# State exchange and a two-layer FFN in float32: batch 1, batch 7 and the state rows move from dense products to block products

## The chip, the cores and the metric

One core of a Trainium2 chip. The metric is the device time in microseconds (us) of one execution, from the runs of the whole program.

## The reference

The attention part reads a state of 32 rows per head and writes it back; the result feeds a two-layer network.

```python
B, H, S, D = x.shape                      # 8, 8, 512, 64; state has 32 rows
a = softmax(scale * x @ state.T)          # over the 32 state rows
xread = a @ state
a2 = softmax(scale * state @ x.T)         # over the 512 tokens
sread = a2 @ x
y = concat([xread, sread], axis=2).transpose(0, 2, 1, 3).reshape(B * 544, 512)
h = y @ w_in                              # 512 x 2048
g = where(h >= 1, h, where(h <= -1, 0, (h + 1) ** 2 / 4))
out = g @ w_out                           # 2048 x 512
```

So there are 8 x 512 token rows and 8 x 32 = 256 state rows. All is float32. TensorE takes each operand as a high and a low part (the low part is the operand less its rounded high part), and each product is three matmuls: high x high, high x low, low x high.

## The kernel before, in words

**First product.** `xread` is never formed. For each batch and each 256 columns of `w_in`, the state is multiplied by `w_in` (small matmuls of 32 x 256, line 639, the S steps), split into high and low (`sw_0h`, `sw_0l`, lines 653 and 655), and multiplied by the attention weights `ath`, `atl` (lines 698 to 700, the U steps). ACT and DVE turn the result into g: `relu` (L707), `square` (L711), `bound` (L715), then, where g feeds a dense product, its high and low part (L724, L730).

**Second product.** Batches 0 and 1 use it densely: `g2` (lines 751 to 753, 192 matmuls of 512 columns a batch, the G steps). Batches 2 to 7 go in pairs (2,3), (4,5), (6,7) through block products in the manner of Strassen and Winograd: per pair 7 products of blocks instead of 8, in two groups of channels g. The Q steps (`quarter`, line 1296, name Q g.k.n) are 336 matmuls of 512 columns a pair. `operand_ops` makes block operands (DVE sums, and a high and a low part each), `weight_ops` loads 1024 KB blocks of W_out (the tile `blocks` in DRAM) through SP, and `done_ops` adds the products up. The 256 state rows come last: their first product has 256 columns (L steps, lines 698 to 700 on `sath`, `satl`), their second is dense (M steps, 96 matmuls of 512 columns), with W_out reloaded by the W steps. `finish` (L764) copies their result out in two parts, one on ACT (L769), one on DVE (L767), and stores each in four pieces of 64 KB from the queues of SP and ACT.

**W_out's block sums.** The D steps (`block_ops`, line 1190) store W_out's split parts in `blocks`, add high and low part on DVE into a work place (`whole`, L1202), make four block sums there (L1208 to L1211), split them (L1214, L1218) and store them too:

```python
nc.vector.tensor_tensor(out=place()[:, :1024], in0=flat[:, 0], in1=flat[:, 1], op=ALU.add)
```

**Attention.** Scores (L480, X steps), then on DVE a 32 x 32 transpose (`turn`, L491), maximum, subtraction, sum, division, transpose back and low part in pieces of 512 elements; the other direction takes a maximum over tokens (`top2`, L560), exchanges through DRAM (`e_there`, `e_x`) and ends in the state read (`read2`, L603, the R steps).

**Order.** The stage of loading (batch 0 and the weights' decoding, lines 781 to 825) follows `ORDER`, a list of numbered operations with their engine. Behind it, `STEPS` lists PE's order step by step, and the class `Flow` places all the other engines' operations around it by costs and buffer rooms. Every engine and every DMA queue works its list in order. `warm` (L401) fills PE with matmuls without a use before the first product.

Of the kernel before, what the change touches and what calls it, by code (L numbers as in the profile page):

```python
# [8 lines left out]
F32 = mybir.dt.float32  # L9
# [9 lines left out]
PAD = 96  # L19
# [297 lines left out]
def state_exchange_moe(  # L317
# [130 lines left out]
    def trade_in(there, name):  # L448

        traded = work.tile([P, NPR, 2 * P], F32, tag="tmp", name=f"{name}_x")  # L450
        for t in range(NT):
            nc.sync.dma_start(
                out=traded[t * NS:(t + 1) * NS], in_=there[:, t].rearrange("(r n) k -> n r k", n=NS)
            )
        return traded

    class Attention:


# [1041 lines left out]
```

## Time and profile before

| what | us |
|---|---|
| runs: lowest, median, highest of 3 | 610.61, 612.99, 613.44 |
| the profiled execution | 610.56 |
| its span, from the first to the last instruction | 608.4 |
| PE, DVE, ACT busy | 600.7, 497.3, 391.5 |
| DMA moved | 122.27 MB, mean 201 GB/s |

The span lies inside the execution's time. An engine's busy time counts each instruction from its start to its modelled end; where they are pipelined, the distance from start to start (the pitch) is shorter than the duration. PEld stands for TensorE's weight loads, SPq for SP's DMA queue. "Idle before" a group names what the engine waited for.

### The profile page before, as it was taken

To read this page: it belongs to the slowest core of one execution; us is meant where nothing else is said; L and a number is where in the kernel's file an instruction comes from. 1 tells how busy PE (TensorE), PEld (TensorE's weight loads), DVE (VectorE), ACT (ScalarE), POOL (GpSimd) and SP (SyncE) were. 2 spreads that over 40 slices of the span, in tenths; PEclk is the share of its full clock that TensorE was granted. 3 is DMA by queue.
4 is the path that set the end of the run, shared out by engine and by line. 5 is a ranking of instruction groups with operands and counts; after the bars stand their busy time and mean duration, and the time that the engine had idled before them with its cause. 6 is when DMAs were issued, how large, how long until landed. Compare 5 with 4: busy or idle time off the path is not lost.

```text
span 608.4 us, 10010 instructions
## 1 busy us (share of the span) xinstructions
PE 600.7 (99%) x4154; PEld 476.6 (78%) x4154; DVE 497.3 (82%) x574; ACT 391.5 (64%) x480; POOL 0.8 (0%) x7
## 2 busy tenths in 40 slices
PE   8999999999999999999999999999999999999997
PEld 3677777787777777878787887788788878888885
DVE  6999985998999999998799849997688484995530
ACT  6999866565589674885566576865656576554520
POOL 0000000000000000000000000000000000000000
PEclk9999999999999999999999999999999999999999
DMA  8997258959474659324587436324646442435971
GB/s 354 424 425 250 69 176 326 371 207 364 149 257 171 229 149 325 81 71 138 163 294 246 129 100 213 105 69 139 208 141 206 139 139 70 138 123 194 358 293 35
DMA packets 65420, 122.27 MB, mean 201 GB/s; under 512 B 2912, under 2 KB 51680, under 8 KB 59232
## 3 DMA queue, kind: packets, MB, share of 16 engines
q1 hardware_dynamic: 65040, 121.32, 56.7%
q8 instruction: 32, 0.52, 0.3%
q10 hardware_dynamic: 336, 0.33, 0.2%
q14 instruction: 12, 0.10, 0.0%
HBM read 91.23 MB, written 30.41 MB: 200 GB/s over the span
## 4 chain that ended last, share of the span: by engine, by line
PE 94%; DVE 2%; ACT 2%; DMA 1%; SPq 0%; issue 0%
PE bank L1296 38%; PE bank L698 11%; PE bank L699 10%; PE bank L700 10%; PE bank L751 6%; PE bank L752 6%; PE bank L753 6%; PE bank L639 5%; PE bank L603 1%; PE bank L480 1%; DMA f<-in_moe_w_in_dram 1%; ACT f L804 1%; ACT f L796 1%; DVE w L812 1%; DVE r L730 0%; DVE one L715 0%
## 5 line engine op out<-in xcount | busy, mean ns | idle before, releaser
L1296 PE MATMUL bank<-r,r 128*128 128x512 f32 x1008 | 238.0, 391 | 0.0
L1296 PEld LDWEIGHTS bank<-r,r 128*128 128x128 f32 x1008 | 188.0, 188 | 44.3 <-issue 4.1
L1262 ACT CAST r<-f 128x1024 fp32r<-128x1024 f32 x84 | 86.9, 1050 | 48.7 <-PE bank L1296 21.8
L707 ACT ACTIVATE f<-bank,half 128x512 f32<-128x512 f32 x104 | 70.9, 687 | 68.3 <-PE bank L700 66.5
L1238 DVE TENSOR_TENSOR r<-f,r 128x1024 fp32r<-128x1024 f32 x84 | 101.3, 1217 | 14.1 <-ACT r L1262 13.8
L715 DVE SCALAR_TENSOR_TENSOR f<-f,bank 128x1024 f32<-128x1024 f32 x52 | 63.0, 1214 | 33.2 <-ACT f L711 33.2
L751 PE MATMUL bank<-r,r 128*128 128x512 f32 x160 | 63.0, 394 | 0.0
L752 PE MATMUL bank<-r,r 128*128 128x512 f32 x160 | 62.3, 389 | 0.0
L753 PE MATMUL bank<-r,r 128*128 128x512 f32 x160 | 62.3, 389 | 0.0
L711 ACT ACTIVATE f<-f 128x1024 f32<-128x1024 f32 x52 | 55.1, 1062 | 1.3
L1330 DVE TENSOR_TENSOR one<-one,bank 128x1024 f32<-128x1024 f32 x30 | 36.4, 1214 | 16.9 <-PE bank L1296 16.1
L1238 DVE TENSOR_TENSOR f<-f,f 128x1024 f32<-128x1024 f32 x36 | 43.4, 1218 | 0.1
L751 PEld LDWEIGHTS bank<-r,r 128*128 128x128 f32 x160 | 30.0, 188 | 9.4 <-issue 2.1
L753 PEld LDWEIGHTS bank<-r,r 128*128 128x128 f32 x160 | 30.0, 188 | 6.4
L752 PEld LDWEIGHTS bank<-r,r 128*128 128x128 f32 x160 | 30.0, 188 | 6.0
L639 PE MATMUL bank<-w,sb 64*32 64x256 f32 x1024 | 32.9, 380 | 1.5 <-DVE w L812 1.0
L639 PEld LDWEIGHTS bank<-w,sb 64*32 64x32 f32 x1024 | 17.6, 106 | 13.4 <-issue 4.0
L707 ACT ACTIVATE one<-bank,half 128x512 f32<-128x512 f32 (+1 forms) x25 | 19.6, 805 | 11.9 <-DVE r L730 8.8
L724 ACT CAST r<-one 128x1024 fp32r<-128x1024 f32 (+1 forms) x17 | 17.0, 999 | 10.4 <-PE bank L752 5.8
L715 DVE SCALAR_TENSOR_TENSOR one<-one,bank 128x1024 f32<-128x1024 f32 (+1 forms) x17 | 19.6, 1150 | 2.2 <-ACT one L711 1.9
L1332 ACT COPY one<-bank 128x1024 f32<-128x1024 f32 x12 | 12.2, 1013 | 13.4 <-PE bank L1296 13.4
L730 DVE TENSOR_TENSOR r<-one,r 128x1024 fp32r<-128x1024 f32 (+1 forms) x17 | 19.7, 1157 | 1.3 <-ACT r L724 1.2
(197 smaller groups left out, 977.1 us busy)
## 6 DMA issues: line engine op xcount, KB each, us to landing
r<-blocks SPq DMA_DIRECT2D x50, 1024.0 KB, 5.8
xt<-in_xt_dram SPq DMA_DIRECT2D x16, 512.0 KB, 6.3
f<-in_moe_w_in_dram SPq DMA_DIRECT2D x8, 1024.0 KB, 10.7
f<-in_moe_w_out_dram SPq DMA_DIRECT2D x8, 1024.0 KB, 14.5
blocks<-r SPq DMA_DIRECT2D x8, 1024.0 KB, 8.9
blocks<-f SPq DMA_DIRECT2D x8, 1024.0 KB, 5.3
xn<-in_x_dram SPq DMA_DIRECT2D x7, 1024.0 KB, 8.8
out_dram<-one SPq DMA_DIRECT2D x12, 512.0 KB, 5.4
```

Source lines behind the costliest of these rows:

```text
L639: nc.tensor.matmul(banks[hh][pr * NS:(pr + 1) * NS, cols], lhsT=sb[rows, b, pr], rhs=w32[c][rows, pr], start=True, stop=True,)
L698: nc.tensor.matmul(o, lhsT=wh[:, k, sl], rhs=ah[:, k], start=first, stop=False)
L699: nc.tensor.matmul(o, lhsT=wl[:, k, sl], rhs=ah[:, k], start=False, stop=False)
L700: nc.tensor.matmul(o, lhsT=wh[:, k, sl], rhs=al[:, k], start=False, stop=last)
L707: nc.scalar.activation(out=u, in_=h, func=AF.Relu, scale=0.5, bias=half)
L715: nc.vector.scalar_tensor_tensor(out=u, in0=u, scalar=1.0, in1=h, op0=ALU.min, op1=ALU.max)
L751: nc.tensor.matmul(a, lhsT=lh, rhs=oh, start=f == 0, stop=False)
L752: nc.tensor.matmul(a, lhsT=lh, rhs=ol, start=False, stop=False)
L753: nc.tensor.matmul(a, lhsT=ll, rhs=oh, start=False, stop=f == NF - 1)
L1238: tt = lambda o, a, b, f: nc.vector.tensor_tensor(out=o, in0=a, in1=b, op=f)
L1262: op(("hi", g, k, half), "ACT", 0.97, lambda: nc.scalar.copy(out=view()[:, 0], in_=value()), need, take=[("win", win)], ends=ends)
L1296: nc.tensor.matmul(o, lhsT=lhs, rhs=v[:, e, a], start=fresh and n == m == 0, stop=n == 3 and m == 2, skip_group_check=not fresh,)
```

## The change

- Batch 1 leaves the dense second product. The pairs are now (1,2), (3,4), (5,6). Batch 7 and the 256 state rows form a block product of their own: 768 rows in two sides of 384 (`SIDE`, `wide`), 336 matmuls of 384 columns. The M and W steps are gone; the state rows' first product (L steps) writes into the block product's bases.
- W_out's high and low part are no longer added on DVE. SP copies the stored high part from `blocks` into the place (`wa`), then POOL adds the stored low part by a DMA that accumulates (`wb`), 512 KB each, eight times; the sums on DVE wait for it.
- Attention pieces of batches 1 to 7 take 1024 elements instead of two of 512. Batch 0 is split by halves of its tokens instead of by halves of its heads.
- The state reads with their exchange are moved: those of batches 0 and 1 out of the loading stage, all of them to other places. The row loads of batches 0 and 1 move with them.
- The warm matmuls run behind the first scores, not ahead of them. `ORDER` and `STEPS` are new.
- The last additions are made in two halves of 384 columns, the second of which ACT's queue stores. The output has another layout, which is undone outside of the timed program.

```diff
-            op(("dA", c), "SP", 2.6, lambda: store_block(0, rounded(wo_at[c]).bitcast(F32)), [("wol", c)], ends=[("wo", c)])
-            op(("wa", c), "DVE", 1.14, whole, [("wol", c), ("send", 0, 3)], take=[("s", ("s", c))], ends=[("wo", c)])
-            op(("ws", c), "DVE", 1.5, sums, [("wa", c)])
+            op(("wa", c), "SP", 1.4, lambda: whole(0), [("dA", c)], take=[("s", ("s", c))])
+            op(("wb", c), "SP", 1.4, lambda: whole(1), [("wa", c)])
+            op(("ws", c), "DVE", 1.4, sums, [("wb", c)])
...
-            def whole():
-                flat = wo[c].rearrange("p e a m -> p e (a m)").bitcast(F32)
-                nc.vector.tensor_tensor(out=place()[:, :1024], in0=flat[:, 0], in1=flat[:, 1], op=ALU.add)
+            def whole(e):
+                (nc.gpsimd if e else nc.sync).dma_start(
+                    out=place()[:, :1024], in_=blocks[g, 0, :, o, e * 1024:(e + 1) * 1024],
+                    **(dict(accum_op=ALU.add) if e else {}),
+                )
...
+        def keep_ops(c):
+            def store():
+                nc.sync.dma_start(out=blocks[c // 4, 0, :, c % 4], in_=rounded(wo_at[c]).bitcast(F32))
+            op(("dA", c), "SP", 2.6, store, [("wol", c)] + ([] if c == NJ - 1 else [("g2", 1, 0, c)]), ends=[("wo", c)])
...
+        SIDE = 3 * P
+        def wide(g):
+            return g >= 6
         def g_of(b, j):
-            return (b - 2) // 2 * 2 + j // 4
+            return (b - 1) // 2 * 2 + j // 4
...
         def block_of(g, side, half, i):
-            return base_of(g, side, half)[:, :, i]
+            if wide(g):
+                return [base_of(g, a, half)[:, i, side * SIDE:(side + 1) * SIDE] for a in range(2)]
+            return [base_of(g, side, half)[:, :, i]]
...
-                    o = chain(g, k)[:, d]
+                    o = chain(g, k)[:, d, :nn(g)]
...
+            cut = [slice(d, d + 1) for d in range(2)] if g == 7 and final else [slice(0, 2)]
...
+                    for d in cut:
+                        (nc.scalar if len(cut) == 2 and d.start else nc.sync).dma_start(out=o[:, d], in_=c[:, d])
...
-        for q in range(2):
-            k = (b, q)
-            if b:
-                op(("turn",) + k, "DVE", 0.62, m("turn", q), [("sc", b)], ends=[("sc", b)])
-                op(("top1",) + k, "DVE", 0.62, m("top1", q), [("turn",) + k])
-                need = [("top1",) + k]
+        if b:
+            op(("turn", b), "DVE", 1.17, m("turn", None), [("sc", b)], ends=[("sc", b)])
...
-    "S1.1.1.2 U1.0 G0.7.0 G0.7.1 U1.1 R1 R0 S1.3.1.4 X2 U1.2 G1.0.0 G1.0.1 U1.3 G1.1.0 S1.5.1.6 "
+    "S1.1.1.2 X2 G0.7.0 U1.0 G0.7.1 U1.1 S2.0.2.1 U1.2 S1.3.1.4 U2.0 U1.3 U2.1 Q0.1.0 Q0.1.1 Q0.2.0 "
...
-    "U7.7 Q4.4.3 Q5.1.0 Q5.1.1 Q5.1.2 Q5.5.0 Q5.1.3 L0 Q5.6.0 Q5.5.1 Q5.5.2 W1.0 Q5.5.3 Q5.6.1 Q5.6.2 "
+    "U7.4 Q6.3.0 Q6.6.3 Q6.3.1 U7.7 U7.6 Q6.3.2 Q6.7.0 Q6.3.3 Q6.7.1 D5 Q6.7.2 U7.5 Q6.7.3 L2 Q6.4.0 "
```

PE at the start of the program. Before (plain is the warm matmuls' operand, xt with sb the scores, w with sb the state times `w_in`, ath with sw the first product):

```order
L401 MATMUL bank<-plain 128x512
L401 MATMUL bank<-plain 128x384
L480 MATMUL bank<-xt_131,sb 32x256 x16
L401 MATMUL bank<-plain 128x512 x6
L401 MATMUL bank<-plain 128x128
L639 MATMUL bank<-w_0_117,sb 32x256 x8
L401 MATMUL bank<-plain 128x512 x3
L401 MATMUL bank<-plain 128x128
L639 MATMUL bank<-w_1_118,sb 32x256 x8
L698 MATMUL bank<-ath_224,sw_0h 128x512
```

PE at the same place now:

```order
L484 MATMUL bank<-xt_127,sb 32x256 x16
L402 MATMUL bank<-plain 128x512
L402 MATMUL bank<-plain 128x384
L402 MATMUL bank<-plain 128x512
L402 MATMUL bank<-plain 128x128
L656 MATMUL bank<-w_0_115,sb 32x256 x8
L402 MATMUL bank<-plain 128x512 x2
L402 MATMUL bank<-plain 128x256
L718 MATMUL bank<-ath_198,sw_0h 128x256
L719 MATMUL bank<-ath_198,sw_0l 128x256
L720 MATMUL bank<-atl_199,sw_0h 128x256
```

The scores have moved to the front and the group on `w_1` is no longer ahead of the first product; it stands behind 12 of the 24 matmuls of 256 columns.

DVE around the W_out sums, before (f<-r is the addition of high and low part, f<-f of 256 the four block sums, of 1024 their low part):

```order
L715 SCALAR_TENSOR_TENSOR one_100<-one_100,bank 128x1024
L541 TENSOR_TENSOR atl_1158<-zt_1139,ath_1157 128x512 x2
L1202 TENSOR_TENSOR f_81<-r_84 128x1024
L1202 TENSOR_TENSOR f_82<-r_88 128x1024
L730 TENSOR_TENSOR r_94<-one_100,r_94 128x1024
L1208 TENSOR_TENSOR f_81<-f_81 128x256
L1209 TENSOR_TENSOR f_81<-f_81 128x256
L1210 TENSOR_TENSOR f_81<-f_81 128x256
L1211 TENSOR_TENSOR f_81<-f_81 128x256
```

DVE around the block sums of the third pair of places now (L1213 to L1216 the four sums, L1223 their low part, L1266 block operands, L744 `bound`, L577 and L501 attention of batch 3):

```order
L1215 TENSOR_TENSOR f_73<-f_73 128x256
L1216 TENSOR_TENSOR f_73<-f_73 128x256
L1223 TENSOR_TENSOR f_78<-f_78 128x1024
L1366 TENSOR_TENSOR one_94<-one_94,bank 128x1024
L1223 TENSOR_TENSOR f_73<-f_73 128x1024
L744 SCALAR_TENSOR_TENSOR f_80<-f_80,bank 128x1024 x2
L1266 TENSOR_TENSOR f_80<-f_80,f_76 128x2x512
L744 SCALAR_TENSOR_TENSOR f_75<-f_75,bank 128x1024
L577 TENSOR_REDUCE nm_3_1227<-bank 128x2
L578 TENSOR_SCALAR nm_3_1227<-nm_3_1227 128x2
L501 STREAM_TRANSPOSE z_1241<-bank 128x1024
L1266 TENSOR_TENSOR r_92<-f_80,r_92 128x1024
```

The additions L1202 are gone; the sums now stand among block operands of the first pair of batches, with the low operand `r_92<-f_80` behind them.

SP in the stretch where W_out's sums are stored, before:

```order
L1198 DMA blocks<-f_81 128x2048
L424 DMA xt_1294<-in_xt_dram 128x1024 x2
L433 DMA xn_1313<-in_x_dram 128x2048
L440 DMA e_3_there<-one_98 128x1024
L1198 DMA blocks<-f_82 128x2048
L452 DMA e_3_x<-e_3_there 32x4x256 x4
```

SP there now (L1204 fetches the high part, L1201 stores the sums, L1305 loads weight blocks, L437 is part of the exchange; POOL's list has eight added rows, `L1204 DMA` into the same places, and nothing else behind its start):

```order
L1201 DMA blocks<-f_73 128x2048
L1201 DMA blocks<-f_81 128x2048
L1204 DMA f_78<-blocks 128x1024
L1204 DMA f_73<-blocks 128x1024
L437 DMA e_2_there<-one_96 128x1024
L1305 DMA r_90<-blocks 128x8x256
L1305 DMA r_82<-blocks 128x8x256
L1201 DMA blocks<-f_78 128x2048
L1201 DMA blocks<-f_73 128x2048
```

The stores of the sums alternate with fetches into the places that they free; loads of weight blocks stand behind these fetches.

## Rows read from the trace of the kernel before

**Rows 1.** The page, part 1: engine, busy us (share of the span), instructions.

```profile
PE 600.7 (99%) x4154; PEld 476.6 (78%) x4154; DVE 497.3 (82%) x574; ACT 391.5 (64%) x480; POOL 0.8 (0%) x7
```

**Rows 2.** Stretches: length, busy us (instructions) of PE, PEld, DVE, ACT, POOL; clock, DMA.

```profile
0.00:17.85 17.85, 14.54 (x90) 5.92 (x91) 11.89 (x26) 12.28 (x18) 0.82 (x7) 1.00 0.89 366
17.85:34.14 16.29, 16.00 (x117) 11.66 (x109) 16.29 (x20) 15.98 (x20) 0.00 (x0) 1.00 1.01 423
34.14:604.32 570.18, 570.16 (x3956) 459.03 (x3956) 468.42 (x529) 363.21 (x444) 0.00 (x0) 1.00 0.55 190
604.32:608.40 4.08, 0.00 (x0) 0.00 (x0) 0.69 (x1) 0.00 (x0) 0.00 (x0) 1.00 0.24 64
```

**Rows 3.** The chain that ended last: start, length, engine, output, line, instructions.

```profile
203.65 2.99 PE bank L1296 x12
...
222.96 2.72 PE bank L1296 x12
...
275.78 8.16 PE bank L1296 x36
```

**Rows 4.** Timeline of PE around the first unit of the state rows: start, length, instruction.

```profile
527.98 0.28 PE L698 MATMUL bank<-sath,wj0h 128*128 128x256 f32 x1
...
533.73 1.09 PE L1296 MATMUL bank<-r,r 128*128 128x512 f32 x4
```

**Rows 5.** Timeline of the head: weight loads, scores, and the first dense second product.

```profile
2.13 0.34 PEld L401 LDWEIGHTS bank<-plain 128*128 128x128 f32 x1 [0.52 <-issue]
...
2.98 0.34 PEld L401 LDWEIGHTS bank<-plain 128*128 128x128 f32 x1 [0.52 <-issue]
...
4.78 0.67 PE L480 MATMUL bank<-xt,sb 64*32 64x256 f32 x16 [0.32 <-DMA sb<-in_state_dram]
...
6.97 0.19 PEld L401 LDWEIGHTS bank<-plain 128*128 128x128 f32 x1 [0.24 <-issue]
...
7.41 0.19 PEld L401 LDWEIGHTS bank<-plain 128*128 128x128 f32 x1 [0.24 <-issue]
...
24.25 0.40 PE L751 MATMUL bank<-r,r 128*128 128x512 f32 x1
```

**Rows 6.** Timeline of DVE around two W_out sums (line 1202).

```profile
121.14 1.28 DVE L523 TENSOR_TENSOR z<-z,s 128x512 f32<-128x512 f32 x2
...
122.34 1.30 DVE L530 STREAM_TRANSPOSE zt<-z 128x512 f32<-128x512 f32 x2
...
126.61 2.46 DVE L1202 TENSOR_TENSOR f<-r 128x1024 f32<-128x1024 f32 x2 [0.48 <-DMA blocks<-f]
128.99 1.22 DVE L730 TENSOR_TENSOR r<-one,r 128x1024 fp32r<-128x1024 f32 x1
```

**Rows 7.** Groups by line and form: busy, mean ns of one, idle before and its releasers.

```profile
L1296 PEld LDWEIGHTS bank<-r,r 128*128 128x128 f32 x1008 | 188.0, 188 | 44.3 <-issue 4.1 <-ACT sw_4h L653 0.8 <-DVE sread L616 0.4
...
L1202 DVE TENSOR_TENSOR f<-r 128x1024 f32<-128x1024 f32 x8 | 9.7, 1217 | 1.0 <-DMA blocks<-f 1.0
...
L791 DVE TENSOR_SCALAR f<-f 128x1024 int32<-128x1024 uint32 x7 | 4.8, 691 | 0.3 <-DMA f<-in_moe_w_out_dram 0.3
```

**Rows 8.** Busy time by stretches, the loading stage's end and behind it.

```profile
45.00:60.00 15.00, 15.00 (x94) 11.80 (x93) 14.93 (x18) 14.94 (x18) 0.00 (x0) 1.00 0.76 269
60.00:150.00 90.00, 90.00 (x716) 70.07 (x715) 77.51 (x111) 58.28 (x78) 0.00 (x0) 1.00 0.67 246
```

**Rows 9.** The DMA view: issues, KB each, median us to landing.

```profile
blocks<-f SPq DMA_DIRECT2D x8, 1024.0 KB, 5.3
...
out_dram<-one SPq DMA_DIRECT2D x12, 512.0 KB, 5.4
...
e_there<-one SPq DMA_DIRECT2D x7, 512.0 KB, 7.6
```

**Rows 10.** Timeline of the tail.

```profile
602.23 3.60 SPq L772 DMA_DIRECT2D out_dram<-one  x4
...
604.34 0.69 DVE L767 COPY one<-bank 128x512 f32<-128x512 f32 x1 [11.62 <-PE bank L753]
```

More of the change, by code (lines that the diff above doesn't have):

```diff
@@ L18 @@
 WARM = 7
-PAD = 96
+PAD = 48
 UNITS = 27
@@ L427, in load_xn @@
     def load_xn(b):
[L428 to L432 removed]
+        xn = work.tile([P, NT, H, D], F32, tag="xn", bufs=1, name=f"xn{b}")
         nc.sync.dma_start(out=xn, in_=x[b])
@@ L455, in trade_in, with flat, some @@
         return traded
+    def flat(a):
+        return a.rearrange("p q s -> p (q s)")
+    def some(q):
+        return slice(None) if q is None else q
     class Attention:
@@ L885, in att_ops1 @@
[L885 to L892 removed]
+        if b:
+            op(("turn", b), "DVE", 1.17, m("turn", None), [("sc", b)], ends=[("sc", b)])
+            keys, n, also = [None], 1.0, []
+        else:
+            for half in range(2):
+                for q in range(2):
+                    op(("turn", b, q, half), "DVE", 0.36, m("turn", q, half), [("sc", b, half)])
+            keys, n = range(2), 0.53
@@ L991, in state_exchange_moe @@
         out_ops(c - 1)
-        if c == 5:
-            read(("xn", 1), 2.6, load, "xn", load_xn, 1, take=[("xn", ("xn", 1))])
     out_ops(NC - 1)
-    weights = [k for k in plan.ops if k[0] == "dma" and k[1] in ("i", "o")]
-    read(("xn", 0), 2.6, load, "xn", load_xn, 0, take=[("raw", ("xn", 0))], after=weights)
     op(("table",), "ACT", 1.3, lambda: nc.scalar.copy(out=pad[:, :1], in_=half))
@@ L1109, in score_ops @@
-            op(("kept", b), "DVE", 1.45, m("turn_traded"), [("trade", b)], take=[(f"r2_{b % 2}", ("r2", b))], ends=[("e2x", b)])
-            for q in range(2):
-                k = (b, q)
-                op(("top1",) + k, "DVE", 0.63, m("top1", q), [("turn",) + k])
-                op(("less1",) + k, "DVE", 0.65, m("less1", q), [("top1",) + k])
-                op(("exp1",) + k, "ACT", 0.54, m("exp1", q), [("less1",) + k])
-                op(("sum1",) + k, "DVE", 0.63, m("sum1", q), [("exp1",) + k])
@@ L1146, in unit_ops @@
             own = unit[k]
-            need = [("swh",) + own, ("swl",) + own] + [(x, b, q) for x in ("ath", "atl") for q in range(2)]
+            g, half = g_of(b, j), j % 4 // 2
+            need = [("swh",) + own, ("swl",) + own]
+            need += [("ath", b), ("atl", b)]
             for i in range(2):
@@ L1250, in operand_ops @@
             elif k == 7:
-                op(("T", g, 3, half), "DVE", 1.14, lambda: tt(s1(), s2(), s1(), ALU.subtract),
+                op(("T", g, 3, half), "DVE", dve, lambda: less(block(1), block(2), block(1)),
                    [("T", g, 2, half), ("hi", g, 1, half), ("lo", g, 1, half)])
@@ L1412, in last_unit @@
-            op(("bound",) + k, "DVE", 1.14, lambda: hid[k].bound(), [("square",) + k], ends=[("h",) + k])
-            op(("gh",) + k, "ACT", 0.97, lambda: hid[k].high(), [("bound",) + k], ends=[("u",) + k],
-               take=[("base", ("g",) + k)])
-            op(("gl",) + k, "DVE", 1.14, lambda: hid[k].low(), [("gh",) + k], ends=[("u",) + k])
-        def last_weights(c, kind):
-            def fetch_wo():
-                t = rounded(flow.place["wob", c])
-                nc.sync.dma_start(out=t.bitcast(F32), in_=blocks[c // 4, 0, :, c % 4])
-                wo[c] = t.rearrange("p (e a m) -> p e a m", e=2, a=2)
-            op(("wob", c), "SP", 2.6, fetch_wo, [("dA", c)], take=[(kind, ("wob", c))])
@@ L1435, in step @@
+        for q in range(2):
+            op(("top2", 0, q), "DVE", 0.82, lambda q=q: atts[0].top2(q),
+               [("aside", 0, q, i) for i in range(2)] + [("top2", 0, 0)] * q)
+            op(("exp2", 0, q), "ACT", 0.7, lambda q=q: atts[0].exp2(q), [("top2", 0, q)])
+        for b in range(2):
+            away_ops(b)
+        for c in range(NC):
+            keep_ops(c)
         def step(g, k, n):
@@ L1471, in _rows @@
 def _rows(y):
-    y = y.copy()
-    for b in range(2, 8):
-        y[b * 544:b * 544 + 512] = y[b * 544:b * 544 + 512].T
-    return y
+    z = y.copy()
+    z[:512] = y[:512]
+    for b in range(1, 7):
+        z[b * 544:b * 544 + 512] = y[b * 512:b * 512 + 512].T
+    last = y[7 * 512:].reshape(512, 768).T
+    z[7 * 544:7 * 544 + 512] = last[:512]
+    for b in range(8):
+        z[b * 544 + 512:b * 544 + 544] = last[512 + b * 32:544 + b * 32]
+    return z
 def kernel(**inputs):
```

433 lines of the change are left out of this document (222 added, 211 removed), and 64 rows, old and new, of tables (ORDER, STEPS).

## Prediction

> **What bounds the kernel now.** I read the page's totals first, then the busy time by stretches, then the chain of waits, then the timelines of the two ends. PE is busy 600.7 of 608.4 us, DVE 497.3, ACT 391.5 [rows 1]. By stretches, PE's 0.29 us without work between 17.85 and 34.14 and 0.02 us between 34.14 and 604.32 are all that it ever waits for; 4.08 us follow with no matmul [rows 2]. So the span is 17.85 us of head, 586.5 us of matmuls end to end, and the tail. The profiled execution took 610.56 us, 2.16 more than its span; the median of the runs shown, 612.99, is 0.4% above it. I sum against 610.56.
>
> What PE costs is therefore the number of matmuls times their pitch. In the chain 36 matmuls of 512 columns take 8.16 us, 0.2267 each [rows 3]; the state rows' 48 matmuls of 256 columns go from 527.98 to 533.73, 0.1198 each [rows 4]. No row has 384 columns: halfway between is 0.1733, three quarters of the longer is 0.1700, one and a half of the shorter 0.1797. I take the halfway value, as it lies between two measured widths. After a stretch of small matmuls the next 12 of 512 columns take 2.99 us where 12 take 2.72, so a return costs 0.27 [rows 3]; I put half of that on an entry.
>
> **TensorE.** Dense second products disappear for batch 1 (192 of 512 columns) and the state rows (96): -288 x 0.2267 = -65.3. The three pairs still have 1008 block matmuls. Batch 7 with the 256 state rows adds 336 of 384 columns: +58.2 (57.1 to 60.4). The first unit of batch 0 becomes 24 of 256 columns for 12 of 512: +0.16. One group of state-weight matmuls moves behind the first product: +0.43. Two more returns and two more entries: +0.8. Sum **-5.7 us** (-6.8 to -3.6). All of it is on the path, as PE never waits.
>
> **Head.** Before, some warm matmuls run ahead of the scores: their weights load at 2.13 and 2.98, 0.85 us apart, in 0.34 us each; behind the scores they load at 6.97 and 7.41, 0.44 apart, in 0.19 [rows 5]. The clock column reads 1.00 (the 2.4 GHz level) in the whole head [rows 2], yet the same instruction takes twice as long with nothing run ahead of it. The change puts the scores first. If they run at the slow pace, 16 of them take 1.3 us instead of 0.67 [rows 5] and DVE's first turn comes 0.6 later; if not, nothing changes. I take the slow pace, because the warm loads are the nearest rows, on the same engine in the same microseconds. DVE's chain from that turn (maxima, exponentials, sums, then the decoding of the weights) sets when sw_0 exists, so it moves with it. In the new order ACT's four copies of the scores stand ahead of the first exponential, and the second half's copies wait until DVE has turned that half. Following PE, DVE and ACT by hand in their new order, with the durations of the same rows, puts the first dense second product at 26.05, where it starts at 24.25 [rows 5]; PE's own list, with the group moved behind 17.85 us, gives 25.0, which the -5.7 holds already. I add **+1.05** (0 to +2.4), 0.6 of it the slow scores.
>
> The Trainium skill, page "TensorE: Matmul & The Clock Gate", Part 1, says that the array's default is throttled and that activity releases the throttle, which speaks against putting the scores first. By it the term is 1.05, by the clock column it is 0.45; the spacing of the loads agrees with the page, and the column does not.
>
> **VectorE.** The pitch of an instruction of 1024 elements is 1.14 to 1.19 us (two take from 126.61 until 128.99), of 512 0.60 (two from 121.14 until 122.34) [rows 6]; for 384 the line through both gives 0.46, and I put 0.47. The eight sums of W_out's halves (1217 ns each [rows 7]) leave DVE: -9. Twelve low parts of dense second products go: -14. Attention's pieces, two of 512 into one of 1024, seven batches and some eight kinds: about -4. The last group's block operands and lows, 88 of 384, add 41, and its additions 9. DVE ends some 23 us fuller. As a total that hides beside PE. But it is not spread evenly: before, DVE is busy 14.93 of 15 us from 45 to 60 and 77.51 of 90 to 150 [rows 8], and the change moves the first pair's block work and its W_out sums into that stretch, while the state reads (a turn each, with their stores, reloads and row loads on SP) move out of it. By hand again, the low part of batch 1's fourth state weights is ready at 107.5 where PE's list, without the head's term, wants it at 106.8, and a low operand behind the block sums of the third pair of places (the second order piece shown) at 144.0 where PE wants it at 141.8. The head's 1.05 covers the first delay and leaves 1.15 of the second's 2.2. I add **+1.2** (0 to +4; DVE's work by hand can be off by 2% of 144 us). After 165 us DVE is 8 us ahead of PE, later 22. In the last group it has 20 us of work beside 25 us of matmuls, so no stall there. ACT gains 56 casts of 384 and stays under 70%: nothing.
>
> **DMA.** The 14 extra weight blocks (1024 KB each), less 8 reads of W_out, plus the two halves of each sum make 14 MB more, in a middle whose DMA share is 0.55 [rows 2]: hidden. The sums are now chains: W_out's split is stored, its high half read back by SP, its low half added by a DMA from POOL, and only then can DVE make the block sums. DVE works in order, so a late sum holds all that is queued behind it, operands that PE waits for among them. SP is in order too: a place of the third pair can be refilled only when its own earlier store has landed, and weight blocks are queued behind that wait. Nearest rows: stores of the same tile land in 5.3 us, 512 KB in 5.4 and 7.6 [rows 9]; before, DVE waited for such a store 1.0 us in all [rows 7]. At these times the sums are ready with 10 and 12 us to spare for the first two pairs of places, 6 for the third, 11 for the fourth. So **0** (0 to +3); less than nothing is excluded, since an earlier sum frees no one who holds PE.
>
> **Tail.** Before, the last copy on DVE runs from 604.34 for 0.69 us, two issues on each queue follow until 605.83 [rows 10], and the span ends 2.57 later. The last block now goes out in two halves: behind the last matmul come an addition of 384 elements, 0.5, one issue on the other queue, 0.4, and a landing, 2.57 if 192 KB take as long as the 64 KB did: 3.5 for 4.08. **-0.6** (-1.0 to +0.5, if the larger store lands a microsecond later).
>
> **Sum.** 610.56 - 5.7 + 1.05 + 1.2 + 0 - 0.6 = **606.5 us**, 0.7% less. About 0.5% (3.05 us) is what a measurement of this kernel can tell from no change: the borders are 607.5 and 613.6. Runs that stand above their profile as those of before do would read up to 609.
>
> **Rivals.** *All is covered.* No slow scores, no late operands: 610.56 - 5.7 - 0.6 = 604.3. For it: the order before leaves PE 0.3 us without work in 586. Against: that order had 12.5 us of DVE's time free between 60 and 150 [rows 8], and this one has less. Chance 0.15.
>
> *DVE becomes the bound early.* The upper ends of the head (+2.4) and DVE (+4) in place of +1.05 and +1.2 give 610.7; half of that 608.6. No change. For it: 14.93 of 15. Against: attention's chains are shorter and the state reads are gone from there. Chance 0.22.
>
> *The accumulating DMA is slow.* If one takes 13 us rather than 5 to 7, the third pair of sums comes 7 us late and the fourth about 2, DVE stands before them, and PE stops once its operands are used up: +9, 615.5; at 20 us, +19, 625. It decides from about 12 us. Against: no 512 KB row is over 7.6 [rows 9]. For it: three transfers now stand in one chain. DVE's double-rate operations could keep POOL from preparing a transfer, but the trace has only seven of 1024 elements, 691 ns each [rows 7], all in the loading stage, ahead of the first sum; that makes this part of it small. Chance 0.15, and 0.03 for other losses.
>
> The Trainium skill, page "SBUF — State Buffer", section "SBUF: two separate sides", has that rule: a DMA issued from GpSimd waits for its descriptors while DVE runs a two-port operation. No run so far shows one.
>
> *A matmul of 384 columns is not cheaper in proportion.* Weight loads are listed at 188 ns [rows 7]; if that were a floor, 336 x 0.188 = 63.2 would shrink the gain to 0.7, and the sum is 611.5. Against: those of 256 columns come every 0.12 us with a load each [rows 4]. Chance 0.02, no change.
>
> **How the numbers follow.** Forecast case 0.43 (604 to 608.5; 0.39 of it below 607.5), all covered 0.15, DVE or the pitch 0.24, slow sums and other losses 0.18. Faster 0.39 + 0.15 = 0.54; slower 0.18; the same 0.28. The range takes in "all covered" with the lower pitch (603) and the first price of the slow sums (615.5); some 0.1 is left out above and under 0.1 below.
>
> **What would show it.** Right: PE busy about 595 us; 384-column matmuls every 0.173; the first dense second product near 26; PE without work for about 1 us between 100 and 150, ended by DVE; the end 3.5 us after the last matmul. Wrong: DVE's block sums waiting for the accumulated tile, or PE idle over 3 us; a pitch off 0.173 by more than 0.005 (1.7 us); a tail as long as before.

## The result, and the profile after

Slower by 0.9%: the median is 617.44 us (614.68 to 619.75, six runs) against 611.86 (610.61 to 613.44, six runs) of the kernel before, a ratio of 1.0089 [1.0059, 1.0118]. The forecast was 606.5. The profiled execution took 619.75, the top of its runs; that of before took 610.56, at the bottom of its. So the spans (618.0 and 608.4) differ by 9.6 us where the medians differ by 5.6, and the waits read below stand somewhat above those of a median run.

The page of the changed kernel, busy time and the DMA queues (packets, MB, share of 16 engines' span; q0 is POOL's queue):

```profile
span 618.0 us, 10299 instructions
...
PE 595.7 (96%) x4208; PEld 481.3 (78%) x4208; DVE 521.4 (84%) x597; ACT 402.3 (65%) x512; POOL 7.8 (1%) x15
...
q1 hardware_dynamic: 79408, 131.28, 61.7%
q0 software_dynamic: 1152, 4.19, 3.7%
```

PE is busy 5.0 us less than before [rows 1], as forecast (about 595), but the span is 9.6 longer. So PE stands still, where before it waited 0.02 us in 570 [rows 2]. The stretches say where (columns as in [rows 2]: length, PE, PEld, DVE, ACT, POOL, clock, DMA share, GB/s):

```profile
60.00:90.00 30.00, 30.00 (x199) 22.96 (x197) 25.13 (x29) 20.46 (x21) 1.88 (x2) 1.00 1.01 356
90.00:120.00 30.00, 24.66 (x149) 18.51 (x149) 26.38 (x35) 23.39 (x33) 1.72 (x2) 0.89 0.80 267
120.00:150.00 30.00, 29.11 (x191) 21.28 (x191) 27.97 (x31) 21.87 (x29) 1.72 (x2) 1.00 0.94 284
...
96.00:100.00 4.00, 4.00 (x11) 3.04 (x11) 2.75 (x4) 0.69 (x1) 0.86 (x1) 0.50 1.01 391
```

DVE has 4.9 us without work from 60 to 90, 4.0 of them ahead of two block sums; PE then loses 5.3 from 90 to 120, and the granted clock falls to 0.50, the 1.2 GHz level. The timeline of DVE in that stretch (L1213 is the first of a place's four block sums, L672 writes the low part of a state weight):

```profile
82.11 1.23 DVE L756 TENSOR_TENSOR r<-one,r 128x1024 fp32r<-128x1024 f32 x1
84.01 0.42 DVE L1213 TENSOR_TENSOR f<-f 128x256 f32<-128x256 f32 x1 [0.67 <-DMA f<-blocks]
...
88.88 0.42 DVE L1213 TENSOR_TENSOR f<-f 128x256 f32<-128x256 f32 x1 [3.31 <-DMA f<-blocks]
...
93.43 1.19 DVE L672 TENSOR_TENSOR sw_1l<-bank,sw_1h 128x1024 fp32r<-128x1024 f32 x1
```

and PE behind it:

```profile
89.73 0.39 PE L781 MATMUL bank<-r,r 128*128 128x512 f32 x1
94.67 0.80 PE L718 MATMUL bank<-ath,sw_7h 128*128 128x512 f32 x1 [4.55 <-DVE sw_1l L672]
95.26 0.63 PE L719 MATMUL bank<-ath,sw_7l 128*128 128x512 f32 x1
...
99.53 0.63 PE L720 MATMUL bank<-atl,sw_7h 128*128 128x512 f32 x1
99.96 0.52 PE L779 MATMUL bank<-r,r 128*128 128x512 f32 x1
```

The two block sums of the first pair of places stand 4.0 us before tiles that are still being added to. The low operand `sw_1l`, the fifth instruction behind the sums in DVE's list, is late by that much, and PE waits 4.55. Then twelve matmuls of 512 columns take 5.29 us (94.67 to 99.96) where twelve take 2.99 after a return [rows 3]: 2.3 us more, at a granted clock of 0.50. It is the only long wait; the other ten between 100 and 605 are 0.35 to 1.17 each, 6.2 in all.

What released DVE: POOL's two issues, and in the chain that ended last the transfer of the second:

```profile
71.91 1.01 POOL L1204 DMA_DIRECT2D f<-blocks  x1 [70.58 <-DVE z L536]
73.10 0.87 POOL L1204 DMA_DIRECT2D f<-blocks  x1 [0.18 <-issue]
...
73.10 15.75 DMA f<-blocks
```

They landed after 12.1 and 15.8 us; the forecast took at most 7.6 [rows 9].

### The profile page after: what moved, and what is told of

The parts are those of the page before. It is cut to its first block, busy times and chain, and to the rows that moved or that the text cites. A ratio compares the mean times of both kernels' runs of the same rounds, so it can differ in the third digit from the quotient of the medians.

```text
span 618.0 us, 10299 instructions
## 1 busy us (share of the span) xinstructions
PE 595.7 (96%) x4208; PEld 481.3 (78%) x4208; DVE 521.4 (84%) x597; ACT 402.3 (65%) x512; POOL 7.8 (1%) x15
## 3 DMA queue, kind: packets, MB, share of 16 engines
q0 software_dynamic: 1152, 4.19, 3.7%
## 4 chain that ended last, share of the span: by engine, by line
PE 73%; DMA 12%; DVE 11%; issue 1%; ACT 1%; POOL 0%; POOLq 0%; DVEq 0%
PE bank L1329 39%; PE bank L718 8%; PE bank L720 8%; PE bank L719 8%; DMA f<-blocks 7%; PE bank L656 3%; DMA r<-blocks 3%; DVE r L1266 2%; DMA blocks<-f 2%; PE bank L779 1%; PE bank L620 1%; PE bank L780 1%; PE bank L781 1%; DVE one L1366 1%; DVE f L1223 1%
## 5 line engine op out<-in xcount | busy, mean ns | idle before, releaser
L1329 PE MATMUL bank<-r,r 128*128 128x512 f32 (+1 forms) x1344 | 301.1, 378 | 4.1 <-DVE r L1266 2.8
L1329 PEld LDWEIGHTS bank<-r,r 128*128 128x128 f32 x1344 | 245.7, 188 | 54.2 <-issue 8.9
L1292 ACT CAST r<-f 128x1024 fp32r<-128x1024 f32 (+1 forms) x140 | 113.1, 835 | 67.7 <-PE bank L1329 36.0
L1266 DVE TENSOR_TENSOR r<-f,r 128x1024 fp32r<-128x1024 f32 (+1 forms) x140 | 129.1, 950 | 10.6 <-ACT r L1292 10.4
L744 DVE SCALAR_TENSOR_TENSOR f<-f,bank 128x1024 f32<-128x1024 f32 x56 | 67.7, 1211 | 26.8 <-ACT f L740 26.8
L1366 DVE TENSOR_TENSOR one<-one,bank 128x1024 f32<-128x1024 f32 (+2 forms) x44 | 46.3, 1058 | 9.7 <-PE bank L1329 8.1
L1266 DVE TENSOR_TENSOR f<-f,f 128x1024 f32<-128x1024 f32 x36 | 43.5, 1214 | 0.1
L1266 DVE TENSOR_TENSOR f<-f 128x384 f32<-128x384 f32 (+1 forms) x44 | 30.8, 732 | 0.1
L779 PE MATMUL bank<-r,r 128*128 128x512 f32 x64 | 25.5, 399 | 0.0
L780 PE MATMUL bank<-r,r 128*128 128x512 f32 x64 | 24.9, 389 | 0.0
L781 PE MATMUL bank<-r,r 128*128 128x512 f32 x64 | 24.9, 389 | 0.0
L718 PE MATMUL bank<-ath,sw_0h 128*128 128x512 f32 (+1 forms) x56 | 21.3, 381 | 1.2 <-DVE one L744 0.8
L720 PE MATMUL bank<-atl,sw_0h 128*128 128x512 f32 (+1 forms) x56 | 21.0, 376 | 0.3 <-DVE atl L557 0.3
L719 PE MATMUL bank<-ath,sw_0l 128*128 128x512 f32 (+1 forms) x56 | 20.9, 374 | 0.0
```

Of the source, the lines that this page charges most:

```text
L718: nc.tensor.matmul(o, lhsT=wh[:, k, sl], rhs=ah[:, k, t], start=first, stop=False)
L719: nc.tensor.matmul(o, lhsT=wl[:, k, sl], rhs=ah[:, k, t], start=False, stop=False)
L720: nc.tensor.matmul(o, lhsT=wh[:, k, sl], rhs=al[:, k, t], start=False, stop=last)
L744: nc.vector.scalar_tensor_tensor(out=u, in0=u, scalar=1.0, in1=h, op0=ALU.min, op1=ALU.max)
L779: nc.tensor.matmul(a, lhsT=lh, rhs=oh, start=f == 0, stop=False)
L1266: nc.vector.tensor_tensor(out=x, in0=y, in1=z, op=ALU.subtract)
```

## The experiments

My theory after the result, A: DMA engines that are full from 45 to 110 us (share 0.98 to 1.02) make the fetch in two transfers late, whatever its form. Rivals, some called B in the texts below: DVE's list had no slack in any case; the accumulating form itself is slow; the head, or the order that the planner (`Flow`) made, is to blame. Ratios are to the kernel before, run beside each.

**The transfer left out** (e5). SP fetches the high part; POOL's transfer is gone, the order of every engine is the same.

```diff
-                (nc.gpsimd if e else nc.sync).dma_start(..., **(dict(accum_op=ALU.add) if e else {}))
+                if not e:
+                    nc.sync.dma_start(out=place()[:, :1024], in_=blocks[g, 0, :, o, :1024])
```

> The changed kernel without POOL's accumulating transfer: the low part of W_out is left out of the block sums (and of them alone), all else and the order on every engine is the same. DVE then waits only for the high part's fetch, which lands near 72. Theory A (the late second leg costs the time): DVE's 8.0 us of waits before the sums go, PE's 4.55 us before 94.67 fall under 1 us, the clock does not fall, and the time is 606 to 610. Rival B (DVE is too full between 60 and 150 in any case): PE still waits over 2 us for DVE between 90 and 120, and the time stays above 612.

610.03 us (608.82 to 610.11), 0.9967 [0.9954, 0.998]: 7.4 less than the changed kernel. No sum waits, PE's wait for `sw_1l` is 0.40, and the clock stays at 1.00. So the eight transfers carry the whole loss; this run does not tell whether by their form or by the traffic that they add.

**DVE or POOL adds instead** (e1, e8). SP fetches both parts, 1024 KB, with one plain load; DVE (e1) or POOL (e8) adds them in place.

```diff
+                    nc.sync.dma_start(out=place(), in_=blocks[g, 0, :, o])
...
+                    nc.gpsimd.tensor_tensor(out=p[:, :1024], in0=p[:, :1024], in1=p[:, 1024:], op=ALU.add)
```

> The changed kernel with one thing undone: SP fetches W_out's high and low part in one plain 1024 KB load, in the place of the high part's fetch in the queue, and DVE adds them in place ahead of the four block sums; POOL moves nothing. Same order on every engine. Theory A (the sums' two transfers in a row land late, DVE stands before the first sums for 4.0 us, PE then 4.55 us and its clock falls): one leg instead of two, the load lands 5 to 8 us after its issue at 66.6, DVE does not wait for it, the idle time of PE before 94.67 shrinks from 4.55 to under 1.5 us, the clock stays up, and in spite of eight additions of 1.14 us on DVE the time falls from 617.4 to 610 to 613. Rival B (DVE is simply too full between 60 and 150 us): with 9 us more on DVE the stalls stay or grow, 617 to 621.

> The changed kernel with another way to the same sum: SP fetches both parts in one plain 1024 KB load (as in the first experiment), and POOL adds them in place by a tensor addition of 1024 elements instead of a transfer; DVE has nothing more to do than in the changed kernel. Theory A: one leg instead of two; if POOL's addition takes under 4 us, both sums are ready before DVE comes to them at 84, no wait, no fall of the clock, 607 to 611. If POOL's addition takes longer than 6 us, or slows DVE's additions beside it, DVE waits again and the time stays at 614 to 620. Rival B: as in the run without the low part, above 612 whatever POOL does.

e1 took 620.06 us, 1.0132 [1.0114, 1.015]; e8 621.97, 1.0161 [1.0133, 1.0189]. With e1 DVE no longer waits before the sums, but its list has two additions of 1.22 us more ahead of `sw_1l`, and PE still waits 2.91 there; the other additions bring waits of their own, the longest 1.95 at 142.58:

```profile
93.16 0.50 PE L718 MATMUL bank<-ath,sw_7h 128*128 128x512 f32 x1 [2.91 <-DVE sw_1l L672]
```

So DVE has no room for eight additions in this order, and e1 could not tell the late transfer from the full list. With e8 POOL's additions hold DVE off. DVE's timeline, then POOL's, then the same two DVE instructions in the changed kernel:

```profile
72.96 6.77 DVE L828 SCALAR_TENSOR_TENSOR wf<-f 128x1024 int32<-128x1024 int32 x2
...
72.90 5.74 POOL L1206 TENSOR_TENSOR f<-f 128x1024 f32<-128x1024 f32 x2 [71.57 <-DMA f<-blocks]
...
72.92 2.36 DVE L828 SCALAR_TENSOR_TENSOR wf<-f 128x1024 int32<-128x1024 int32 x2
```

They take 6.77 us instead of 2.36, and PE then waits 2.6 us twice for low parts of state weights. The Trainium skill, page "SBUF — State Buffer", section "SBUF: two separate sides", says that a GpSimd operation that reads SBUF and a DVE operation with two SBUF inputs exclude one another; this row agrees.

**The head** (e4). The warm matmuls ahead of the scores again.

```diff
-    "84A 0S 1S 86P 89D ... 10S 85P 102D "
+    "84A 85P 0S 1S 86P 89D ... 10S 102D "
```

> The changed kernel with the first warm matmuls ahead of the scores again. If the scores run at the slow pace because nothing runs ahead of them, the first 16 take 0.67 us again and the first dense second product starts 0.4 to 0.8 us earlier than 25.57; if the pace has another cause, it starts within 0.2 us of 25.57. The time itself moves by less than can be measured, 616 to 618.

619.83 us, one run. Its scores and its first dense second product:

```profile
4.74 2.21 PE L484 MATMUL bank<-xt,sb 64*32 64x256 f32 x32 [0.26 <-DMA sb<-in_state_dram]
...
25.51 0.50 PE L779 MATMUL bank<-r,r 128*128 128x512 f32 x1
```

In the changed kernel these are 2.15 and 25.57, so in this run the place of the warm matmuls changed neither. The scores one by one (ns: least, median, most), before, in the changed kernel and in e4:

```profile
L480 PE MATMUL bank<-xt,sb x32: 376/388/400, 4.8 to 6.1; 64*32 64x256 f32 x32
...
L484 PE MATMUL bank<-xt,sb x32: 630/631/632, 4.8 to 6.3; 64*32 64x256 f32 x32
...
L484 PE MATMUL bank<-xt,sb x32: 627/631/632, 4.7 to 6.3; 64*32 64x256 f32 x32
```

The scores of the changed kernel are slow, as the prediction took them to be, but with the warm matmuls ahead they are as slow. So it is not shown that running first is what slows them; e4 is one trace, and what else does it stays open.

**The planner told the truth** (e2, e3). e2 raises the lateness that the planner assumes for the two legs, and the planner reorders.

```diff
+    CHAIN = {"wa": 5.0, "wb": 10.0}
...
-        return self.LATE[self.ops[k][0]]
+        return self.CHAIN.get(k[0], self.LATE[self.ops[k][0]])
```

> The changed kernel with the same instructions; only the planner is told that the two legs of a sum land 5 and 10 us after their issue instead of 2.6 and 2.6, so that DVE's list has the block sums further back, behind other work. Theory A: DVE no longer stands before the sums (8.0 us of waits in 5 places become under 2), PE's 4.55 us before 94.67 go and the clock stays up: 609 to 612. Rival B: DVE's work is the same, so is the time, 616 to 619. Rival C (what follows the sums, their stores and the weight blocks, is late then): the wait moves to PE before block products, ended by DMA of weight blocks, 614 to 620.

> The changed kernel with one wait more: the four stores of W_out's second half (1024 KB each, issued from 68.8 us on) wait on SP until the first two accumulating transfers have landed. Same order on every engine. Theory A1 (the accumulating transfers are late since up to 6 MB of stores and weight blocks stand in the same 16 engines): they land 6 to 9 us after their issue instead of 12.1 and 15.8, DVE waits under 1 us, PE's 4.55 us shrink to under 1.5, the time falls to 609 to 613. Theory A2 (an accumulating transfer issued by POOL is slow by itself): still 11 us or more, 616 to 620 with the later stores. Rival B: no difference in PE's waits, 616 to 619.

e2: 633.8, 1.0356 [1.0335, 1.0376]. Other work came ahead: PE waits 2.12, 3.98 and 4.17 for DVE and 1.81 for ACT; a miss. e3's edit, meant to hold the places apart, gave the same program, instruction for instruction: 617.03, 1.0079 [1.0052, 1.0107]. So it tests nothing, but as a second trace of the changed kernel it shows the same wait: 4.33 us of PE before 94.59.

**Loads moved out of the way** (e11 to e14). In e11 the first two weight blocks go behind the first stored block sums on SP, and a row load of batch 1 behind batch 0's exchange:

```diff
+        for k in (('wt', 0, 2), ('wt', 0, 1)):
+            flow.order.remove(k)
+            flow.order.insert(flow.order.index(('dS', 3)) + 1, k)
...
```

> The changed kernel with three loads moved back in SP's list and nothing else: the two first weight blocks (1024 KB each) stand behind the first store of block sums instead of ahead of the second half's W_out stores, and the row load of batch 1 (1024 KB) behind batch 0's exchange store. Same order on all other engines. Theory A1 (the accumulating transfers share the 16 DMA engines with up to 6 MB that were issued around them): the fetch lands earlier, the two accumulating transfers take 6 to 10 us instead of 12.1 and 15.8, DVE waits under 1 us for the first two sums, PE's 4.55 us shrink to about 0.4, the clock stays up, and the time is 609 to 613. Theory A2 (an accumulating transfer is slow by itself): still 11 us or more, 616 to 619. If weight blocks are then late for the first block products: PE waits there by DMA, 613 to 618.

> As the kernel before it, and the 1024 KB of batch 4's tokens, which stand ahead of the seventh sum's transfers, move behind the fifth weight block of the first group. Theory A1: the wait of 2.82 us at 167.6 goes as well, and with it some 1.6 us of PE: 607.5 to 611.5, at best the 610.0 of the kernel without the low part or a little under it. Rival B sets the floor: DVE has no slack, so the 0.3 to 0.7 us waits that stay in the kernel without the low part stay here. If the tokens come too late for batch 4's scores, DVE and PE wait there instead.

> The changed kernel with four loads moved back in SP's list, all other engines' orders untouched: the first two weight blocks one behind each of the second pair's fetches, batch 3's tokens behind batch 0's output, batch 1's rows behind the weight block of the sixth product. The two runs with loads moved showed that the first pair's transfers then land in 7 to 9 us and the wait goes to the second pair, whose fetch stood behind 2 MB. Theory A1 (the late sums are a matter of what is issued just ahead of them on the same DMA engines): here both pairs are on time, DVE's waits before the sums between 80 and 125 fall from 4.0 (changed kernel) and 7.8 (loads moved) to under 2 us, PE loses under 3 us in 90 to 120, and the time is 609 to 612. If the stretch is simply full (DMA share 0.93 to 1.0 between 45 and 120), the wait moves to the weight blocks or to the third pair: 613 to 619.

> As the kernel before it, with batch 4's tokens moved back as well and the first maximum of batch 0's state direction (0.83 us on DVE) put behind the split of batch 1's second state weights, which PE waits for. Rival B (no slack on DVE): PE's first wait near 90, 0.4 us and 0.27 for the matmul behind it, goes; the later ones stay. 608.5 to 611.5, under the kernel before it by 0 to 1.5 us.

e11 took 621.4, 1.0166 [1.0137, 1.0194]. Its DVE timeline:

```profile
83.36 0.42 DVE L1213 TENSOR_TENSOR f<-f 128x256 f32<-128x256 f32 x1
...
84.82 0.42 DVE L1213 TENSOR_TENSOR f<-f 128x256 f32<-128x256 f32 x1
...
110.36 0.42 DVE L1213 TENSOR_TENSOR f<-f 128x256 f32<-128x256 f32 x1 [2.56 <-DMA f<-blocks]
...
118.24 0.43 DVE L1213 TENSOR_TENSOR f<-f 128x256 f32<-128x256 f32 x1 [5.20 <-DMA f<-blocks]
```

The first pair's accumulations now land in 7.1 and 7.9 us and nobody waits for them; the second pair's sums wait instead (7.8 us), and PE 2.22 and 4.87. There both links are late: SP's plain fetches, behind the loads moved ahead of them, landed after 10.5 and 14.1 us, the accumulations after 9.1 and 9.0. Further spreading shrinks this: e12 (batch 4's tokens later too) 619.63, 1.0131 [1.0108, 1.0155]; e13 (one weight block behind each fetch of the second pair) 618.92, 1.0118 [1.009, 1.0146]; e14 (e13 with part of batch 0's maximum moved behind a low state weight and batch 4's tokens later) 618.4, 1.0105 [1.009, 1.0119], still with a wait of 3.81 at the fourth sum (113.53). None gets below the changed kernel (617.44; the intervals of e12, e13 and e14 overlap its own): four misses. So competition for the DMA engines decides which transfers are late. That still fits theory A and the rival that the form is slow.

**POOL adds and the order changed** (e10): e8 with batch 0's two maxima over tokens (`top2`) held behind a low state weight, and the planner's order made anew.

> As the kernel in which POOL adds, and the two maxima of batch 0's state direction (top2, 0.83 us each), which nobody needs soon, may only come behind the split of batch 1's fourth state weights; the planner orders DVE, ACT and SP anew with that. If what is left is DVE's in-order list with no slack (rival B's part), PE's waits between 90 and 120 shrink by up to 1.7 us against the kernel without this: 605 to 610. If the new order puts other work in front of what PE needs, it is the same or slower by some us.

634.23, 1.0357 [1.0329, 1.0384]: operands from DVE late again (PE's longest waits for it 4.1, 3.1 and 2.8). A miss, and no way to a faster kernel.

**The same transfer, written instead of added** (e15). This one decides.

```diff
-                    **(dict(accum_op=ALU.add) if e else {}),
```

> The transfer from POOL's queue writes the low part over the high part instead of adding to it: same bytes, same queue, same order on every engine, no addition (the block sums are then sums of the low part alone). Theory A (the DMA engines are full from 45 to 110 us, and any transfer of 512 KB issued at 72 us lands late): landings of the first pair stay at 11 to 16 us, DVE still stands 3 to 4 us before the sums, the time stays within 2 us of the changed kernel, 615.5 to 619.5. Rival B (adding in memory is itself slow in a full stretch, because each element is read at the target first): first pair lands in 6 to 9 us, DVE waits under 0.5 us, no low clock between 92 and 100, time 610 to 612.5.

610.46 us (608.87 to 617.86, ten runs, the second highest 613.70), 0.9995 [0.9964, 1.0025]. Theory A as it was stated, that any transfer issued there lands too late whatever its form, falls: with the same bytes, queue and order, 7.0 us are gone. From its page, its stretches and its DVE timeline:

```profile
q0 software_dynamic: 1152, 4.19, 2.0%
...
76.00:80.00 4.00, 4.00 (x20) 3.30 (x19) 4.00 (x5) 2.82 (x3) 0.00 (x0) 1.00 1.07 408
80.00:84.00 4.00, 4.00 (x20) 3.30 (x18) 3.95 (x6) 2.11 (x2) 0.00 (x0) 1.00 1.04 425
...
83.49 0.42 DVE L1213 TENSOR_TENSOR f<-f 128x256 f32<-128x256 f32 x1
...
84.96 0.42 DVE L1213 TENSOR_TENSOR f<-f 128x256 f32<-128x256 f32 x1
```

The changed kernel in the same stretches:

```profile
76.00:80.00 4.00, 4.00 (x19) 3.30 (x19) 4.00 (x5) 2.71 (x4) 0.00 (x0) 1.00 1.09 270
80.00:84.00 4.00, 4.00 (x20) 3.30 (x19) 3.33 (x3) 1.97 (x2) 0.00 (x0) 1.00 1.07 298
```

At a like share of busy DMA engines, 1.07 to 1.09 and 1.04 to 1.07, the accumulating kernel moves about a third less. For the same 4.19 MB POOL's packets take 3.7% of 618.0 us, 22.9, against 2.0% of 607.3, 12.1: 1.9 times as long. The first pair lands in 7.8 and 10.3 us instead of 12.1 and 15.8, just in time.

The records of the single DMA packets in the two traces say the same without the crowd: a packet of 4096 bytes on POOL's queue takes 327 or 328 ns (median) where it accumulates and 159 where it writes, alike in 70 to 92, 95 to 120 and 120 to 180 us; e17, which has both forms (its plain ones are stores in the loading stage), shows 327 and 159. And POOL is not late to begin: the first packet comes 4.5 us behind the first issue where it adds, 4.1 where it writes. So the other reason that the prediction weighed, POOL held off by DVE while it prepares a transfer, does not make the difference.

The Trainium skill, page "Collectives: The Full Stack", section "Stop ④ — SDMA + CCE: where bytes move and the add happens", tells of the addition in the DMA path, for collectives, as reading twice and writing once, with the add free in between. The runs do not part the second read from the add; what they show is the price of both together: the DMA holds the engines nearly twice as long as one that writes. The crowd counts too: with loads moved away (e11) the same two accumulations landed in 7.1 and 7.9 us. The loss needed both the form and what was queued around it.

**An exact program with fewer accumulations** (e16 to e18). W_out as decoded, `wf`, is the sum of both parts. POOL's queue stores it while the loading stage decodes it, and SP fetches it with one plain transfer.

```diff
+        if kind == "o" and c < JOINED:
+            nc.gpsimd.dma_start(out=joined[c], in_=a)
...
+                    nc.sync.dma_start(out=place()[:, :1024], in_=joined[c])
```

> W_out as decoded is already the sum of its high and low part. For the first six of the eight places POOL's queue stores it (512 KB, plain, while it is being decoded), and SP fetches it with one plain transfer instead of fetching the high part and accumulating the low part; the last two places fetch both parts and DVE adds them (1.14 us each, in a stretch where DVE had slack). Nothing accumulates in memory. Theory (the accumulating form is what costs; the traffic as such does not): DVE does not wait at the sums, the first stall of TensorE near 90 is 0.4, the clock stays at 1.00, and the time is that without the low part, 609 to 612. Rival (the loading stage, whose DMA share is 1.0, pays for 3 MB more): first product or a decoding step is late, TensorE stalls 1 to 5 us before 80, 613 to 617.

> As the kernel with six joined places, but only the first pair of places is fetched joined; the other six accumulate as in the changed kernel. If nearly all of the 7 us comes from the first pair: 610 to 612.5, sums of the first pair without a wait, later ones waiting under 1 us each. If the six later accumulations carry a share of their own (as when loads were moved away from the first pair): sums of the second pair wait 2 to 5 us near 110, 614 to 619.

> The first two pairs of places fetched joined, the last four accumulate. If the full stretch to about 120 us is what makes an accumulation dear, these four cost nothing: 609 to 612, as with six joined; any wait left is at the seventh sum (it waited 2.8 us in the changed kernel), under 1 us of TensorE's time. If accumulating costs wherever it stands: 2 to 4 us over the kernel with six joined.

| joined places | accumulating | us | ratio |
|---|---|---|---|
| none (the change) | 8 | 617.44 | 1.0089 [1.0059, 1.0118] |
| 2 (e17) | 6 | 612.56 | 1.0009 [0.9988, 1.0029] |
| 4 (e18) | 4 | 610.93 | 0.9986 [0.9966, 1.0007] |
| 6, DVE adds the last two (e16) | 0 | 611.88 | 1.001 [0.9994, 1.0027] |

The places are filled in the order 3, 1, 2, 0, so e17's two joined places are one of the first pair and one of the second, not the first pair as its expectation has it. One accumulation fewer in each of the first two pairs gives back 4.9 of the 7.0 us; its remaining one in the first pair landed in 11.1, and PE waited 1.19 at 91.23 instead of 4.55 (the trace of e17 is of a fast run, 609.75). The four after 120 us in e18 hold DVE 1.3 before one sum, and PE waits 1.10; yet e18 is not measurably slower than e16, which has none, though the DMA share is 0.96 from 120 to 150. So the dear ones are the first four, and one fewer in each of their pairs already takes most of the loss away; between e17 and e18 the intervals overlap. Waits of PE in e18:

```profile
90.79 0.50 PE L721 MATMUL bank<-ath,sw_7h 128*128 128x512 f32 x1 [0.40 <-DVE sw_1l L675]
104.64 0.50 PE L721 MATMUL bank<-ath,sw_0h 128*128 128x512 f32 x1 [0.41 <-DVE sw_0l L675]
108.04 0.50 PE L721 MATMUL bank<-ath,sw_3h 128*128 128x512 f32 x1 [0.36 <-DVE sw_3l L675]
136.85 0.46 PE L721 MATMUL bank<-ath,sw_4h 128*128 128x512 f32 x1 [1.10 <-DVE one L1375]
226.16 1.63 PE L1338 MATMUL bank<-r,r 128*128 128x512 f32 x6 [1.53 <-DMA r<-blocks]
595.89 9.63 PE L1338 MATMUL bank<-r,r 128*128 128x384 f32 x54 [1.48 <-DMA r<-blocks]
```

The 3 MB more that e16 stores in the loading stage did no harm before 80 us, against the rival. None of the exact versions is measurably faster than the kernel before; e18 has the lowest median, 6.5 us under the changed kernel.

## Why the prediction was wrong, point by point

**DMA, "0 (0 to +3)": the step that failed.** "At these times the sums are ready with 10 and 12 us to spare for the first two pairs of places" took landings from [rows 9], medians over the whole program, most of it less full. The term was 0 with at most +3; by the medians of the changed kernel and e15 the accumulations alone cost 7.0. In the first pair's stretch both links were longer. The stores of the split parts, issued from 48.01, landed like this:

```profile
DMA to landing us min/median/max: 9.9/13.3/16.4
```

16.4 where 5.3 was taken, 11.1 more; so SP's fetches start at 66.56. The accumulation took 15.8 where 7.6 was the dearest row, 8.2 more. Together this is more than the 10 us to spare (how these were worked out is not on record, so the two cannot be set off to the microsecond). The late stores alone were bearable, as e15 shows with the same stores (up to 16.8); the accumulating form is the rest. My reason for a low price, that no 512 KB row is over 7.6, came from plain transfers only. "A middle whose DMA share is 0.55" hid the same thing: the share is 1.01 from 60 to 90. And nearer rows stood on the page of the kernel before, which the prediction left aside: the stores of these very split parts, and loads of the full loading stage.

```profile
f<-in_moe_w_out_dram SPq DMA_DIRECT2D x8, 1024.0 KB, 14.5
blocks<-r SPq DMA_DIRECT2D x8, 1024.0 KB, 8.9
```

**The rival "slow accumulating DMA"** (0.15, 615.5 at 13 us) named the form, the wait and nearly the time, but put it at the third pair; it came at the first, which has DVE's full list behind it. Its price left out the 2.3 us at the lower clock, so that its 615.5 lies near the measured 617.44 is in part luck.

**TensorE, -5.7: right within its range.** The last group's matmuls of 384 columns, and the first dense second product:

```profile
25.57 0.50 PE L779 MATMUL bank<-r,r 128*128 128x512 f32 x1
...
580.75 23.05 PE L1329 MATMUL bank<-r,r 128*128 128x384 f32 x132
```

23.05 by 132 is 0.1746 with the last one's full length in it; 0.1733 was taken. "PE busy about 595" came out (595.7) with the slow clock's 2.3 us in it; e15, without them, has 592.9. That hit is luck. e15 has the same work without the late tiles: 609.1, 1.46 under the profile of before. Of that, +0.8 is its head (25.81 against 25.0 from PE's own list), +2.1 waits for DVE, +1.3 for weight blocks, -0.7 the tail (3.35 us for 4.08); that leaves -4.9, restarts after six waits in it (0.27 each). Some 0.4 of it lies outside the span (1.8 us are left beside it in e15, 2.16 before), so -4.5 is TensorE's, still between -6.8 and -3.6.

**Head, +1.05: about half of it came, inside its range; its reason is not shown.** 25.57 against 26.05 is 0.57 behind PE's own list. The slow scores did come: the first 16 take 1.11 us for 0.67, and DVE's first turn starts 1.24 behind the first score where it was 0.80, so 0.44 of the 0.6. But e4 has them as slow behind the same warm matmuls, so that the scores run first is not shown to be why. The clock column reads 1.00 in all three heads and does not show the slow pace at all. The rule on the throttled default, cited in the prediction from the Trainium skill, cannot tell these traces apart: behind the same warm matmuls the scores ran fast in one and slow in the other.

**VectorE, +1.2: too low by 0.9.** e15's waits for DVE are 0.40, 0.41, 0.37, 0.26 and 0.70, five small ones rather than the two worked out, all between 90 and 152.

**Weight blocks, in the same 0: 1.3 us** in e15 (1.00 at 225.71, 0.25 at 594.35), 3.0 in e18. The 14 MB more are not quite hidden; before, PE waited 0.02 us in all.

**Tail, -0.6: right.** PE ends at 614.60, the span 3.4 later.

Without the loss of the accumulations the forecast's other steps give 606.5 and e15's profile 609.1. So the forecast gain would have failed without it too: by medians e15 is level with the kernel before (0.9995). The 2.6 us between 606.5 and 609.1 are the low terms for DVE and the weight blocks, and a TensorE gain 0.8 smaller (with the 0.4 outside the span counted to it), less 0.2 for the head and 0.1 for the tail.

## What to carry to other kernels

Take a transfer's landing time from the stretch in which it will run, with the traffic that the change adds there, not from a median over the program; and price a DMA that adds as nearly two that write. Before an addition is moved from an engine into a DMA, look at what is queued behind its result: here 4 us on an engine without slack became 4.55 on PE and 2.3 more at the lower clock. Where the sum exists already somewhere (here as decoded, before the split), store it there and fetch it plainly; here that gave back the loss, not a gain over the kernel before.

## What the runs showed of the hardware

- A DMA that accumulates into SBUF holds the DMA engines 1.9 times as long as one of the same bytes that writes (22.9 and 12.1 us for 4.19 MB; 327 or 328 against 159 ns for a packet of 4096 bytes, in crowded stretches and others alike). POOL's issue is longer too, 0.86 to 1.01 us against 0.53 to 0.67. In a stretch with DMA share 1.0 two of them landed in 12.1 and 15.8 us, in one with fewer loads around them (e11, share 0.93) in 7.1 and 7.9.
- After a wait of 4.55 us the clock was granted at 0.50 until about 100 us; e11's wait of 4.87 left 0.90 as the mean of 120 to 150. The length of one wait does not tell it alone: e1's wait of 2.91 at 93.16 was followed by 1.00 from 96 to 100, its wait of 1.95 at 142.58 by 0.50 from 144 to 146.
- The clock column can read 1.00 where matmuls run slow: the scores are listed at 631 ns in all 16 traces of the changed kernel and its variants, 388 before, all at 1.00.
- A POOL addition of two SBUF tiles holds DVE's two-input operations off: 6.77 us for two that take 2.36. POOL's eight additions of 1024 elements took 2.40 to 3.37 us each beside DVE.
- Not settled: how much of an accumulation's longer hold is the second read and how much the addition, and whether an accumulation in DRAM costs the same. Neither was tried.
